# Per-head sums of squares of six batches in four 32-column matmul tiles, one activation, and a spread over partitions by transfers, in a linear attention and gated convolution kernel

## The chip, the cores and the metric

The kernel runs on one core of one Trainium2 chip. The metric is the device time of one execution in microseconds (us); lower is better. TensorE is called PE below, VectorE DVE, ScalarE ACT, GpSimd POOL and SyncE SP, as the profile does. PE's results land in PSUM, from which DVE and ACT take them to SBUF; transfers are issued by SP (plain copies and transposes) and by POOL (loads that change the type).

## The reference

There are 8 batches, 8 heads, 576 rows and 64 columns per head.

```python
kv  = einsum('bhsd,bhse->bhde', k, v)            # per head 64 x 64
o   = einsum('bhsd,bhde->bhse', q, kv)
rms = sqrt(mean(o * o, axis=-1, keepdims=True) + 1e-06)      # per batch, head and row
x   = o / rms * g_norm                            # then heads side by side: (8, 576, 512)
x1, x2, x3 = split(x @ w_proj, 3, axis=-1)
conv = irfft(rfft(x2, axis=1) * rfft(filter_fft, axis=0), n=576, axis=1)
out  = (x1 * conv * x3) @ w_out
```

The change touches how `1 / rms` comes about: it is one number for each batch, head and row, and it multiplies the 64 columns of that head.

## The kernel before

Everything is bf16 on PE with sums in float32. A batch is held with the 512 columns (8 heads of 64) on partitions, as four column blocks j = 0 to 3 of 128 partitions, so two heads lie in one block, and with the 576 rows along the free dimension in two halves of 288 (`TH`). The steps of a batch b, by the names that the code gives them:

- `K` sums k and v to kv, `eK` brings it to SBUF; `Qt` transposes q by a transfer of SP's (line 405; the first two batches use PE, `T0` and `T1`), and `Qh` is a tiny copy on POOL that waits for it.
- `O01` and `O23` (line 454) are attention outputs, two blocks each, in PSUM. ACT squares them (`sq`, line 464) and copies them with the gain g (`ob`, line 471; `ov` on DVE in batch 0).
- `R0` to `R3` (line 461) sum the squares of each head: two matmuls of 288 columns for each block, with `ind`, a 128 x 128 matrix of two blocks of ones, as weights. So the sum of a head appears on all of its 64 partitions. `rs0` to `rs3` (line 475, ACT) turn it to 1/rms in the tile `rstd`. `x0` and `x1` (line 489, DVE) multiply two blocks each of `o` by `rstd`; `x0` needs blocks 0 and 1, `x1` blocks 2 and 3.
- `Ga` and `Gb` (line 627) are the projections for x1 and x3, eight matmuls of 288 columns for each of four blocks, `x1n` and `gn` their evictions on ACT (633) and DVE (635). `fd`, `fr`, `fa` fold x on DVE, `rrM`, `rrT`, `abM`, `abT` project the folded x2 (lines 530 to 550), `F0` to `F2t` transform it, `M0` to `M2` (602, 617) multiply by the filter's spectrum, `A0`, `A1` (608) add products on POOL, `Av` on DVE. `Io`, `I`, `os`, `u`, `w`, `fin` transform back and multiply by the gates, `U`, `U4`, `ot` (750, 763, 754) apply `w_out` and store by transfers of SP's (757, 770).

All steps of all batches stand in one string, `ORDER`, each word a step and a batch (`R2.5` is step R2 of batch 5; a third number is a count of idle matmuls ahead of it). A loop walks it and each step issues its instructions on its engines, so the string sets the order on every engine and in every queue. Batches overlap: the attention part of batch b+1 runs among the convolution of batch b. Four tiles of two PSUM banks go round (`take` and `free`), and `sq`, `o` and `rstd` exist once each, so a batch's `rstd` may be written only when `x0` and `x1` of the batch ahead have read it. SP and POOL have semaphores for eight transfers each, so a transfer waits for the one eight ahead of it in its queue.

Of the kernel before, what the change touches and what calls it, by code (L numbers as in the profile page):

```python
# [19 lines left out]
ORDER = """Z.0 Zi.0 Lg.0 Lkb.0 Zt.0 Lq.0 Lvb.0 Lva.0 An.0 Lka.0 Zd.0 Zf.0 Lf.0 Tg.0 Zp.0 T0.0.20 Act.0 eTv0.0 T1.0 Lw1.0 Kb.0  # L20
eKb.0 Tb2.0 eTv1.0 Tb1.0 Lq.1 Lw2.0 Tb0.0 O23.0 sq2.0 Ka.0 R2.0.1 sq3.0 eKa.0 ov2.0 O01.0 rs2.0 ov3.0 sq1.0 R3.0 ov1.0
sq0.0 R1.0.1 rs3.0 rs1.0 x1.0 R0.0 ov0.0 rs0.0 x0.0 Ff2.0 Ff0.0 fd0.0 Ff1.0 Ga0.0 fr0.0 fr1.0 Lw3.0 fa0.0 Ga1.0 x11.0
Lv.1 fd1.0 x10.0 H1.0 H0.0 rrM.0 Lk.1 fa1.0 T0.1 rrT.0 err.0 eTa0.1 H2.0 Gb1.0 HN0.0 HN1.0 abM.0 F0.0 Gb0.0 eab.0 g1.0
K.1 M0.0 T1.1 abT.0 Lk.2 g0.0 eK.1 O01.1 eTa1.1 eT.0 sq0.1 ob0.1 F2.0 F2t.0 M2.0 sq1.1 Ga2.0 Lv.2 Lq.2 x12.0 Gb2.0
ob1.1 R1.1 g2.0 rs1.1 F1.0 R0.1 F1t.0 O23.1 rs0.1 sq2.1 Ga3.0 ob2.1 sq3.1 M1.0 R2.1 rs2.1 x0.1 ob3.1 x13.0 Av1.0 A0.0
Gb3.0 g3.0 R3.1 rs3.1 Lq.3 Qt.2 K.2 eK.2 Io01.0 I01.0 x1.1 Ga1.1 fd.1 Ga0.1 os01.0 u01.0 x11.1 Io23.0 O01.2 fr.1 x10.1
os23.0 sq0.2 I23.0 sq1.2 rrM.1 Qh.2 ob0.2 u23.0 ob1.2 Qt.3 R0.2 fa.1 rs0.2 w.0 rrT.1 err.1 O23.2 fin.0 abM.1 sq2.2
ob2.2 F0.1 eab.1 sq3.2 abT.1 eT.1 Gb1.1 Gb0.1 ob3.2 F1.1 M0.1 g1.1 R2.2 F1t.1 Lv.3 g0.1 rs2.2 Lk.3 R3.2 Ga3.1 rs3.2
R1.2 x13.1 Lwo.0 K.3 Lk.4 rs1.2 M1.1 Gb3.1 A0.1 x1.2 F2.1 Lv.4 x0.2 eK.3 A1.1 O23.3 F2t.1 g3.1 sq3.3 sq2.3 M2.1 fd.2
fa.2 U0.0 Io01.1 ob3.3 ob2.3 os01.1 ot0.0 Ga2.1 I01.1 x12.1 Gb2.1 R3.3 Io23.1 u01.1 rs3.3 g2.1 os23.1 I23.1 O01.3  # L30
abM.2 Lq.4 u23.1 w.1 sq1.3 sq0.3 Qh.3 Lq.5 Ga0.2 fin.1 ob1.3 ob0.3 abT.2 eab.2 x10.2 Ga1.2 R1.3 eT.2 fr.2 R0.3 x11.2
Gb1.2 rs1.3 F1.2 R2.3 rs0.3 F1t.2 g1.2 rrM.2 rs2.3 F2.2 rrT.2 K.4 M1.2 Qt.4 Lk.6 F2t.2 U2.0 eK.4 Lv.6 Lk.5 Lv.5 err.2
x1.3 Ga3.2 x0.3 M2.2 O23.4 ot2.0 x13.2 F0.2 sq3.4 sq2.4 ob2.4 Lq.6 ob3.4 fr.3 U0.1 M0.2 Qt.5 Gb0.2 R2.4 g0.2 Gb3.2
ot0.1 rs2.4 A1.2 A0.2 R3.4 g3.2 rrM.3 rs3.4 Io01.2 rrT.3 I01.2 os01.2 err.3 I23.2 Ga2.2 Gb2.2 fd.3 x12.2 fa.3 u01.2
g2.2 Io23.2 os23.2 u23.2 abM.3 abT.3 U4.1 eab.3 Ga0.3 ot4.1 F1.3 eT.3 w.2 fin.2 x10.3 O01.4 sq1.4 ob1.4 Qh.4 F1t.3
M1.3 sq0.4 U2.1 Ga1.3 ob0.4 ot2.1 F0.3 K.5 x1.4 A1.3 x11.3 F2.3 Gb0.3 eK.5 F2t.3 M0.3 R0.4 g0.3 Ga2.3 rs0.4 x12.3 R1.4
Gb2.3 M2.3 O23.5 rs1.4 Gb1.3 g2.3 x0.4 sq3.5 A0.3 sq2.5 ob3.5 ob2.5 U0.2 Io01.3 I01.3 Qt.6 fd.4 g1.3 fa.4 Ga3.3 os01.3
Gb3.3 x13.3 u01.3 Io23.3 g3.3 fr.4 abT.4 ot0.2 O01.5 os23.3 I23.3 eT.4 sq0.5 ob0.5 u23.3 Lk.7 abM.4 sq1.5 K.6 ob1.5
w.3 Ga0.4 eab.4 F1.4 R2.5 eK.6 x10.4 F1t.4 rs2.5 R3.5 rs3.5 rrM.4 R0.5 rs0.5 F2.4 fin.3 M1.4 x1.5 rrT.4 F2t.4 err.4
Ga1.4 R1.5 Gb1.4 M2.4 x11.4 Lv.7 rs1.5 O23.6 g1.4 sq3.6 F0.4 U2.2 sq2.6 ob3.6 Qh.5 Ga3.4 M0.4 ob2.6 ot2.2 O01.6 x13.4  # L40
Gb3.4 sq1.6 x0.5 Gb0.4 ob1.6 A1.4 g3.4 sq0.6 R3.6 ob0.6 A0.4 rs3.6 g0.4 U4.3 Ga2.4 ot4.3 R2.6 Gb2.4 fr.5 x12.4 rs2.6
fd.5 Io01.4 R1.6 I01.4 g2.4 os01.4 rrM.5 Io23.4 rs1.6 rrT.5 u01.4 os23.4 err.5 K.7 x1.6 I23.4 R0.6 Zn.0 fa.5 u23.4
abM.5 abT.5 rs0.6 eK.7 eab.5 U2.3 Lq.7 F0.5 Ga0.5 Qt.7 ot2.3 w.4 F1.5 fin.4 eT.5 F2.5 x10.5 M0.5 A0.5 F1t.5 U0.4 x0.6
M1.5 ot0.4 F2t.5 M2.5 A1.5 U0.3 Gb0.5 ot0.3 O23.7 sq3.7 g0.5 Ga1.5 Gb1.5 ob3.7 x11.5 fd.6 Io01.5 Ga2.5 fa.6 sq2.7 g1.5
I01.5 ob2.7 Ga3.5 os01.5 Io23.5 fr.6 x12.5 x13.5 Gb3.5 u01.5 Gb2.5 I23.5 os23.5 g3.5 g2.5 abM.6 Ga0.6 u23.5 eab.6
x10.6 O01.7 sq0.7 abT.6 ob0.7 eT.6 sq1.7 w.5 rrM.6 ob1.7 F1.6 Qh.6 rrT.6 F2.6 F1t.6 fin.5 err.6 F2t.6 U0.5 M1.6 Ga1.6
A1.6 F0.6 ot0.5 R2.7 M2.6 R1.7 x11.6 rs2.7 Gb0.6 U4.5 rs1.7 M0.6 R0.7 Gb1.6 A0.6 ot4.5 g0.6 R3.7 rs0.7 Ga2.6 U2.4
rs3.7 g1.6 I01.6 x12.6 Io01.6 Gb2.6 ot2.4 x1.7 Ga3.6 x0.7 fr.7 os01.6 u01.6 g2.6 rrM.7 fd.7 fa.7 x13.6 Io23.6 I23.6
os23.6 Gb3.6 g3.6 rrT.7 Ga1.7 err.7 abM.7 x11.7 u23.6 eab.7 F0.7 Ga0.7 x10.7 abT.7 w.6 F1.7 M0.7 eT.7 fin.6 Gb0.7 g0.7
F1t.7 F2.7 Ga2.7 x12.7 A0.7 F2t.7 Gb1.7 M1.7 U2.5 Av1.7 Qh.7 M2.7 g1.7 U2.6 Gb2.7 vae0.6 Io01.7 vve1.6 I01.7 ot2.5  # L50
g2.7 dse0.6 Ga3.7 dge1.6 J3.7 os01.7 x13.7 uj3.7 J2.7 dge2.6 uj2.7 U0.6 Gb3.7 u01.7 w01.7 dae3.6 fin01.7 wo23.7 wm23.7
Vq0.7 ot0.6 U4a.7 g3.7 fo23.7 U4b.7 vau.7 fm23.7 dsu2.7 Vq2.7 Vp0.7 dgu1.7 vaq0.7 vvq1.7 dsu0.7 dgu3.7 Vp2.7 dgq1.7
dsq0.7 dsq2.7 vap0.7 daq3.7 vvp1.7 dgp3.7 dap1.7 dsp0.7 dgp2.7"""


@with_exitstack
def kernel(
# [400 lines left out]
    def R(b, j):  # L458
        r2 = tmp['r', b, j] = take(("r", b, j))
        for h in range(2):  # L460
            nc.tensor.matmul(r2[:, h, 0:TH], ind, sq()[:, j, h * TH:(h + 1) * TH], start=True, stop=True)  # L461
# [416 lines left out]
```

## Time and profile before

| | us |
|---|---|
| median of 3 runs | 218.33 (218.29 to 219.61) |
| the profiled execution | 219.81 |
| its span, first to last instruction | 218.0 |
| PE busy in it | 200.0 |
| DVE, ACT, POOL busy in it | 184.0, 147.4, 68.1 |
| mean granted PE clock | 0.987 |

The profiled execution took 1.81 us more than its span and 1.48 us more than the median. A row of the timeline gives start and duration of neighbouring equal instructions (x8 is eight of them), their line and tiles, and in brackets how long their engine had stood idle and what ended it. Matmuls are pipelined: the start of the next row, not the end of the last, tells how long a row kept PE.

### The profile page before, as it was taken

Reading aid. Unit: us, or ns where it says so; the run is one execution under the profiler, and the core shown is the slowest. Engines: PE = TensorE matmul, PEld = TensorE weight load, DVE = VectorE, ACT = ScalarE, POOL = GpSimd, SP = SyncE. Lnnn points to the kernel's source line nnn. Section 1 sums busy time; section 2 is a strip of 40 time slices with the busy share of each in tenths; the row PEclk is TensorE's granted clock in tenths of the full one; section 3 lists DMA queues with packets and bytes.
Section 4 is the critical chain, followed back from the end, with each engine's and each line's share of the span. In section 5 each row is a group of like instructions: output and inputs, shape, how many; then the busy total and the mean of one; then the engine's idle time right before and its main releaser. Section 6 shows DMA issues by size and latency. Waiting matters only on the chain.

```text
span 218.0 us, 4583 instructions
## 1 busy us (share of the span) xinstructions
PE 200.0 (92%) x1825; PEld 123.2 (57%) x1848; DVE 184.0 (84%) x275; ACT 147.4 (68%) x232; POOL 68.1 (31%) x67
## 2 busy tenths in 40 slices
...
GB/s 64 203 208 206 205 204 203 187 182 163 205 174 146 230 86 146 230 156 191 240 147 188 121 0 98 154 115 96 164 32 0 38 111 96 0 3 18 178 205 132
DMA packets 40810, 30.12 MB, mean 138 GB/s; under 512 B 15796, under 2 KB 36276, under 8 KB 40788
## 3 DMA queue, kind: packets, MB, share of 16 engines
...
q8 instruction: 14, 0.23, 0.4%
...
HBM read 33.69 MB, written 9.44 MB: 198 GB/s over the span
## 4 chain that ended last, share of the span: by engine, by line
PE 69%; DVE 15%; DMA 5%; issue 3%; ACT 3%; POOL 1%; POOLq 0%; DVEq 0%; ACTq 0%
PE ps L627 24%; PE ps L750 10%; PE ps L544 5%; DMA wp<-in_moe_w_proj_dram 5%; DVE tpw L602 4%; PE ps L654 4%; PE ps L530 3%; PE ps L550 3%; PE ps L461 3%; PE ps L380 2%; PE ps L537 2%; PE ps L454 2%; PE ps L763 1%; PE ps L569 1%; PE ps L576 1%
## 5 line engine op out<-in xcount | busy, mean ns | idle before, releaser
L627 PE MATMUL ps<-x,wp 128*128 128x288 bf16 x512 | 72.5, 288 | 2.9 <-DVE tpw L602 2.4
L608 POOL TENSOR_TENSOR Y<-tpw 97x1024 bf16<-97x1024 f32 (+1 forms) x14 | 36.9, 2638 | 100.9 <-DVE tpw L602 100.8
L627 PEld LDWEIGHTS <-wp 128*128 128x128 bf16 x512 | 48.9, 98 | 21.5 <-issue 6.0
L602 DVE TENSOR_TENSOR tpw<-ps,HH 97x2048 f32<-97x2048 f32 (+1 forms) x16 | 36.6, 2288 | 3.6 <-PE ps L583 1.9
L635 DVE TENSOR_TENSOR g<-ps,x 128x576 bf16<-128x576 f32 x32 | 24.0, 753 | 8.3 <-PE ps L627 6.5
L475 ACT ACTIVATE rstd<-ps,bias_eps 128x576 bf16<-128x576 f32 x32 | 23.1, 748 | 7.5 <-PE ps L461 7.5
L633 ACT CAST x<-ps 128x576 bf16<-128x576 f32 x32 | 20.5, 644 | 10.9 <-PE ps L627 10.4
L750 PE MATMUL ps<-wo,yg 128*128 128x512 bf16 x106 | 26.0, 379 | 0.6 <-DVE g L635 0.2
L554 ACT CAST x<-ps 128x1024 bf16<-128x1024 f32 (+1 forms) x24 | 21.0, 874 | 8.2 <-PE ps L544 5.2
L464 ACT ACTIVATE sq<-ps 128x576 bf16<-128x576 f32 x32 | 20.1, 657 | 1.8 <-PE ps L454 1.6
L471 ACT ACTIVATE o<-ps,g_col 128x576 bf16<-128x576 f32 x28 | 20.3, 753 | 0.0
L754 ACT COPY ot<-ps 128x1024 f32<-128x1024 f32 x13 | 13.2, 1018 | 7.9 <-PE ps L750 7.8
L750 PEld LDWEIGHTS <-yg 128*128 128x128 bf16 x112 | 10.7, 98 | 12.1 <-issue 0.5
L654 PE MATMUL ps<-IV,Y 128*128 128x192 bf16 x120 | 15.6, 246 | 0.0
L544 PE MATMUL ps<-wp,ab 128*128 128x512 bf16 x58 | 14.8, 379 | 0.4
L663 DVE TENSOR_TENSOR u<-ps,os 128x576 bf16<-128x576 f32 x15 | 11.3, 754 | 3.1 <-ACT os L658 1.5
L461 PE MATMUL ps<-sq,ind 128*128 128x288 bf16 x64 | 13.0, 291 | 0.9 <-DVE o L469 0.5
L658 ACT COPY os<-ps 128x576 f32<-128x576 f32 x15 | 9.6, 642 | 5.5 <-PE ps L655 3.8
L655 PE MATMUL ps<-IV,Y 97*128 97x96 bf16 x60 | 12.4, 207 | 0.0
L489 DVE TENSOR_TENSOR x<-o,rstd 128x1152 bf16<-128x1152 bf16 x16 | 11.8, 750 | 0.7 <-ACT rstd L475 0.6
L386 ACT CAST kvblk<-ps 64x256 bf16<-64x256 f32 (+2 forms) x25 | 8.8, 353 | 4.5 <-PE ps L380 4.3
L654 PEld LDWEIGHTS <-Y 128*128 128x128 bf16 x120 | 9.6, 98 | 3.3 <-issue 1.1
...
## 6 DMA issues: line engine op xcount, KB each, us to landing
out_dram<-ot SPq DMA_DIRECT2D x54, 128.0 KB, 2.4
...
vb<-in_v_dram POOLq DMA_DIRECT2D x7, 576.0 KB, 10.7
kb<-in_k_dram POOLq DMA_DIRECT2D x7, 576.0 KB, 12.2
wp<-in_moe_w_proj_dram POOLq DMA_DIRECT2D x3, 512.0 KB, 11.4
...
```

The lines of the kernel that those rows point to most:

```text
L464: act.activation(out=halves(sq()[:, j]), in_=tmp['o', b, j][:, :, 0:TH], func=AF.Square)
L471: act.activation(out=by_time(osb(), j), in_=i_, func=AF.Copy, scale=g_col)
L475: act.activation(out=by_time(rstd(), j), in_=by_row(tmp['r', b, j]), func=AF.Abs_reciprocal_sqrt, scale=1.0 / D, bias=bias_eps)
L544: nc.tensor.matmul(pp[:, h], abt()[:, j, 2 * h * P:(2 * h + 1) * P], w2(j), start=(j == 0), stop=(j == NDC - 1))
L554: act.copy(out=o_(), in_=tmp[key, b])
L602: vec.tensor_mul(out=t_[:n], in0=xp[:n].unsqueeze(1).to_broadcast([n, 2, 2, DM]), in1=two)
L608: op(out=Yt()[:n, 2 * g:2 * g + 2], in0=t_[:n, ::-1, 0], in1=t_[:n, ::-1, 1])
L627: nc.tensor.matmul(pp[:, h, 0:TH], w_, x[:, j, h * TH:(h + 1) * TH], start=(j == 0), stop=(j == NDC - 1))
L633: act.copy(out=x1, in_=pp[:, :, 0:TH])
L635: vec.tensor_mul(out=halves(g13t()[:, dc]), in0=pp[:, :, 0:TH], in1=x1)
L654: nc.tensor.matmul(pp[:, i, 0:SB], Y[:, 2 * g + h, cs], IV[:, 2 * g + h, 0:SB], start=(g == 1), stop=(g == 2))
L750: nc.tensor.matmul(pp[:, cc], ygt(b)[:, dc, b % 2 * 64 + c * P:b % 2 * 64 + (c + 1) * P], wo[:, dc], start=(dc == 0), stop=(dc == NDC - 1))
```

## The change

For batches 1 to 6 the four pairs of `R` matmuls and the four `rs` activations are replaced. `Rc` issues eight matmuls with `ind32`, 128 x 32 weights whose 16 left columns are ones for the upper head and whose 16 right columns are ones for the lower; block j goes to column tile 32j of PE and to partitions 32j to 32j+31 of one PSUM tile. So all eight heads stand in one PSUM tile, 16 equal partitions each. `rsc` is one activation over it to the new tile `rc`. Then `sp0` to `sp3` spread it: for each head, one transfer on SP's queue reads one partition of `rc` 64 times over and writes 64 partitions of `rstd` (576 bf16 each, 73.7 KB), two for each block and eight for each batch, 48 in all. Batches 0 and 7 keep `R` and `rs`. `ORDER` is another string throughout; the loads of batch 1's q, k and v now stand ahead of those of `w_proj`.

```diff
-eKb.0 Tb2.0 eTv1.0 Tb1.0 Lq.1 Lw2.0 Tb0.0 O23.0 sq2.0 Ka.0 R2.0.1 sq3.0 eKa.0 ov2.0 O01.0 rs2.0 ov3.0 sq1.0 R3.0 ov1.0
+sq2.0 eTv0.0 ov3.0 Lka.0 Lva.0 Lq.1 R3.0.1 rs3.0 ov2.0 Tb0.0 Ff1.0 Ff0.0 Ka.0 eKa.0 Tb1.0 R2.0 Lk.1 Lv.1 rs2.0 Zp.0
...
+    ind32 = consts.tile([P, 32], BF16)
...
+        vec.memset(ind32, 0.0)
+        for h in range(2):
+            vec.memset(ind32[64 * h:64 * h + 64, 16 * h:16 * h + 16], 1.0)
...
+    rc = lambda: buf("rc", 0, [P, S])
+
+    @one
+    def Rc(b):
+        r2 = tmp['rc', b] = take(("rc", b))
+        for h in range(2):
+            for j in range(NDC):
+                nc.tensor.matmul(r2[32 * j:32 * j + 32, h, 0:TH], ind32, sq()[:, j, h * TH:(h + 1) * TH], start=True, stop=True,
+                                 tile_position=(0, 32 * j))
+
+    @one
+    def rsc(b):
+        act.activation(out=rc().rearrange("p (m a r) -> p a m r", m=3, a=2), in_=by_row(tmp['rc', b]),
+                       func=AF.Abs_reciprocal_sqrt, scale=1.0 / D, bias=bias_eps)
+        free(("rc", b))
+
+    def spread(b, j):
+        for hp in range(2):
+            r = rc()[32 * j + 16 * hp:32 * j + 16 * hp + 1]
+            nc.sync.dma_start(out=rstd()[64 * hp:64 * hp + 64, j:j + 1], in_=bass.AP(tensor=r.tensor, offset=r.offset, ap=[list(r.ap[0]), [0, 64], [1, S]]))
+
+    for j in range(NDC):
+        step["sp%d" % j] = lambda b, j=j: spread(b, j)
```

PE in batch 5, before: the sums of one block stand between other matmuls, and the other blocks' pairs follow some steps on (`sq` are the squares, `ind` the ones; `x_481,FY` is part of `F1` of batch 4).

```order
L576 MATMUL ps_69<-x_481,FY 128x512
L461 LDWEIGHTS ind
L461 MATMUL ps_67<-sq,ind 128x288
L461 LDWEIGHTS ind
L461 MATMUL ps_67<-sq,ind 128x288
L583 LDWEIGHTS FZ
```

After, at the same place (lines have moved by 32): all eight stand in one run, each of 32 output partitions, behind `abT` (`wp,ab`) and ahead of `F1` (`x_620,FW`) of batch 4. Two of the eight are shown.

```order
L582 MATMUL ps_66<-wp,ab 128x512
L478 LDWEIGHTS ind_83
L478 MATMUL ps_69<-sq,ind_83 32x288
...
L478 LDWEIGHTS ind_83
L478 MATMUL ps_69<-sq,ind_83 32x288
L608 LDWEIGHTS FW
L608 MATMUL ps_68<-x_620,FW 128x512
```

So four short stretches of full-width matmuls became one stretch per batch, for which PE changes to 32-column tiles and back.

SP before, from the queue's start: the transposes of q of batches 2 and 3 stand ahead of everything, then stores.

```order
L182 DMA g_row<-in_g_norm_dram 1x2x64
L405 DMA_TRANSPOSE qT<-qb_74 128x24x96 [waits DMASW6_49,DVE_49,PE_49]
L405 DMA_TRANSPOSE qT<-qb_75 128x24x96 [waits DMASW7_49,DVE_49,PE_49]
L757 DMA out_dram<-ot 64x1x512 [waits Activation_49]
```

After, from the last spread of batch 1 on: the transpose for batch 2, then the four transfers of `sp3` and `sp2` of batch 2, then the transpose for batch 3 (it waits for POOL's load of q), and only behind it `sp1` and `sp0` of batch 2.

```order
L490 DMA rstd<-rc 64x1x576 [waits DMAHW0_49]
L413 DMA_TRANSPOSE qT<-qb_74 128x24x96 [waits DMAHW1_49,DMASW3_49,PE_49]
L490 DMA rstd<-rc 64x1x576 [waits DMAHW2_49,Activation_49]
L490 DMA rstd<-rc 64x1x576 [waits DMAHW3_49]
L490 DMA rstd<-rc 64x1x576 [waits DMAHW4_49]
L490 DMA rstd<-rc 64x1x576 [waits DMAHW5_49]
L413 DMA_TRANSPOSE qT<-qb_75 128x24x96 [waits DMAHW6_49,DMASW0_49,PE_49]
L490 DMA rstd<-rc 64x1x576 [waits DMAHW7_49,DVE_49]
L490 DMA rstd<-rc 64x1x576 [waits DMAHW0_49]
L490 DMA rstd<-rc 64x1x576 [waits DMAHW1_49]
L490 DMA rstd<-rc 64x1x576 [waits DMAHW2_49]
L789 DMA out_dram<-ot 64x1x512 [waits DMAHW3_49,Activation_49]
```

So the second half of batch 2's `rstd` moved behind a transpose and its load.

DVE where batch 1's x is made, before: both parts of x follow `M1` or a gate of batch 0, next to the activations that feed them.

```order
L602 TENSOR_TENSOR tpw<-ps_66,HH 128x2048
L489 TENSOR_TENSOR x<-o,rstd 128x1152
L608 TENSOR_TENSOR Y<-tpw 128x1024
L635 TENSOR_TENSOR g_532<-ps_66,x_432 128x576
L489 TENSOR_TENSOR x<-o,rstd 128x1152
```

After: two gates and `M0` of batch 0 stand between the activation `rsc` of batch 1 and its first x, which now waits for four transfers, and `M1` of batch 0 (L634, 128x2048), `M2` (L649) and gates stand behind it.

```order
L667 TENSOR_TENSOR g_631<-ps_66,x_557 128x576
L667 TENSOR_TENSOR g_631<-ps_67,x_547 128x576
L634 TENSOR_TENSOR tpw<-ps_68,HH 97x2048
L521 TENSOR_TENSOR x<-o,rstd 128x1152
L634 TENSOR_TENSOR tpw<-ps_67,HH 128x2048
L649 TENSOR_TENSOR Y<-ps_69,HM 128x1024
L640 TENSOR_TENSOR Y<-tpw 128x1024
L667 TENSOR_TENSOR g_631<-ps_68,x_547 128x576
L521 TENSOR_TENSOR x<-o,rstd 128x1152
```

So x moved away from the activation that feeds it, and a wait there now holds up products of the batch ahead.

More of the change, by code (lines that the diff above doesn't have):

```diff
@@ L24 @@
[L24 to L53, printed above, removed]
+ORDER = """Z.0 Lg.0 Lkb.0 Lq.0 Zi.0 Lvb.0 Zt.0 Zd.0 T0.0.22 An.0 Lf.0 Act.0 Zf.0 T1.0 Kb.0 Tg.0 eKb.0 eTv1.0 Tb2.0 O23.0 sq3.0
@@ new lines @@
+sq2.0 eTv0.0 ov3.0 Lka.0 Lva.0 Lq.1 R3.0.1 rs3.0 ov2.0 Tb0.0 Ff1.0 Ff0.0 Ka.0 eKa.0 Tb1.0 R2.0 Lk.1 Lv.1 rs2.0 Zp.0
+Ff2.0 O01.0 T1.1 sq1.0 eTa1.1 Lw1.0 sq0.0 ov1.0 ov0.0 Lw2.0 H2.0 T0.1 R1.0 rs1.0 eTa0.1 H1.0 x1.0 fd1.0 R0.0 K.1 eK.1
+rs0.0 x0.0 H0.0 O01.1 sq0.1 Ga0.0 sq1.1 ob0.1 fd0.0 ob1.1 fa1.0 x10.0 Ga1.0 x11.0 fa0.0 O23.1 Lq.2 sq3.1 Lw3.0 fr0.0
+sq2.1 fr1.0 ob2.1 abM.0 ob3.1 Rc.1 rrM.0 rrT.0 rsc.1 Gb1.0 err.0 HN0.0 Gb0.0 g1.0 eab.0 g0.0 sp3.1 F0.0 abT.0 F2.0
+HN1.0 sp2.1 sp1.1 Lv.2 F1.0 M0.0 eT.0 sp0.1 F1t.0 F2t.0 Qt.2 Lk.2 x1.1 Ga2.0 x12.0 M1.0 A0.0 Ga3.0 x13.0 Lv.3 Gb2.0
@@ new lines @@
+M2.0 K.2 Av1.0 g2.0 Gb3.0 Io01.0 x0.1 eK.2 O01.2 os01.0 g3.0 I01.0 sq0.2 Lq.3 ob0.2 Ga1.1 sq1.2 u01.0 ob1.2 fr.1 x11.1
+Io23.0 os23.0 Ga0.1 fd.1 x10.1 O23.2 I23.0 rrM.1 sq3.2 u23.0 rrT.1 sq2.2 Qh.2 ob2.2 Rc.2 ob3.2 fa.1 Lwo.0 Gb1.1 w.0
+rsc.2 abM.1 sp3.2 abT.1 fin.0 err.1 sp2.2 eab.1 F0.1 Qt.3 Lk.3 F1.1 eT.1 g1.1 Ga3.1 x13.1 F1t.1 M0.1 K.3 F2.1 A0.1
+eK.3 Gb0.1 M1.1 F2t.1 g0.1 Ga2.1 Gb2.1 x12.1 sp1.2 M2.1 g2.1 O23.3 sq3.3 U0.0 x1.2 sq2.3 sp0.2 ob3.3 A1.1 Io01.1 ob2.3
+I01.1 Io23.1 os01.1 Gb3.1 x0.2 fd.2 ot0.0 Ga1.2 u01.1 g3.1 O01.3 os23.1 fa.2 x11.2 I23.1 u23.1 sq0.3 sq1.3 abM.2 ob0.3
```

39 lines of the change are left out of this document (31 added, 8 removed).

## The prediction

> **What bounds the kernel now.** I read the page's busy times first, then the chain that ended last, then the busy times by stretches.
>
> ```profile
> span 218.0 us, 4583 instructions
> PE 200.0 (92%) x1825; PEld 123.2 (57%) x1848; DVE 184.0 (84%) x275; ACT 147.4 (68%) x232; POOL 68.1 (31%) x67
> PE 69%; DVE 15%; DMA 5%; issue 3%; ACT 3%; POOL 1%; POOLq 0%; DVEq 0%; ACTq 0%
> ```
>
> PE is busy for 92% of the span and is 69% of the chain. The stretches (length, then PE, PEld, DVE, ACT and POOL busy, then PE's clock, DMA share and GB/s) show where that holds:
>
> ```profile
> 13.00:25.00 12.00, 9.63 (x114) 5.16 (x112) 10.24 (x28) 10.17 (x18) 5.66 (x8) 1.00 1.21 205
> 45.00:55.00 10.00, 9.19 (x123) 5.92 (x117) 9.78 (x18) 9.44 (x18) 3.26 (x5) 1.00 1.17 181
> 85.00:95.00 10.00, 7.67 (x50) 4.66 (x48) 7.73 (x9) 4.87 (x8) 4.15 (x3) 0.83 1.23 207
> 165.00:175.00 10.00, 9.95 (x69) 5.29 (x68) 8.34 (x7) 8.21 (x12) 2.37 (x1) 1.00 0.15 36
> ```
>
> From about 95 us on PE has 9.95 of 10 us: a microsecond of PE work taken out there is a microsecond of span. Between 45 and 55 us DVE has 9.78 of 10 and PE has gaps, with the transfer engines full (1.17 of their time): there DVE and transfers count. The stretch at 85 us holds one accident, used below.
>
> **The removed matmuls.** The first row is PE's group of `R`, the second ACT's group of `rs`.
>
> ```profile
> L461 PE MATMUL ps<-sq,ind 128*128 128x288 bf16 x64 | 13.0, 291 | 0.9 <-DVE o L469 0.5 <-ACT rstd L475 0.3
> L475 ACT ACTIVATE rstd<-ps,bias_eps 128x576 bf16<-128x576 f32 x32 | 23.1, 748 | 7.5 <-PE ps L461 7.5
> ```
>
> 291 ns is the latency of one matmul; what a pair keeps PE from is read off the starts in the timeline:
>
> ```profile
> 68.67 0.41 PE L461 MATMUL ps<-sq,ind 128*128 128x288 bf16 x2
> 68.92 0.33 PE L654 MATMUL ps<-IV,Y 128*128 128x192 bf16 x2
> ```
>
> A pair takes 68.92 - 68.67 = 0.25 us, four pairs 1.00 us. `Rc` also has eight matmuls of 288 columns, in two rounds of four column tiles. Do four such tiles run side by side? The filter's folding (L305) issues 32-column tiles of 512 columns already:
>
> ```profile
> 19.40 0.40 PE L305 MATMUL ps<-fn,rev 96*32 96x512 bf16 x4
> 19.62 0.40 PE L305 MATMUL ps<-fn,ident 96*32 96x512 bf16 x4
> ```
>
> Four start every 0.21 us, 0.41 ns a column, so two rounds of 288 take 0.24 us. But PE must change its tiling and back:
>
> ```profile
> 62.12 1.16 PE L627 MATMUL ps<-x,wp 128*128 128x288 bf16 x8
> 63.20 0.41 PE L590 MATMUL ps<-x,FZ 128*64 128x512 bf16 x2
> 63.54 0.44 PE L454 MATMUL ps<-qT,kvblk 64*64 64x288 bf16 x8
> ```
>
> Eight gate matmuls keep PE for 0.98 us (the chain, below), so the tiled L590 could start at 63.10 and starts at 63.20: 0.10 lost going in. Its two run side by side, 0.21 us, so the next could start at 63.41 and starts at 63.54: 0.13 lost. `Rc` costs 0.24 + 0.23 = 0.47 us for 1.00, and six batches save 6 x 0.53 = 3.2 us. The bounds: without the two changes 6 x 0.76 = 4.6 us saved; if tiles do not overlap, 8 x 0.125 + 0.23 = 1.23 us, 1.4 us lost over six batches. I take 3.2, since the fold is the same tile width. The Trainium skill, TensorEngine Tiling (Array Packing), Key Properties, says that changing the tiling mode drains TensorE; by that the 0.23 belongs in, and the two gaps agree. Taken without it the sum would be 4.6.
>
> **The removed activations.** 18 x 0.748 = 13.5 us leave ACT. ACT is 68% busy and PE waited for `rstd` only twice (0.3 us each, in the waits), so PE's work hides them: 0, bound 0.6 us gained. A gain for DVE or PSUM beyond that I cannot see in the waits.
>
> **The transfers.** 48 new ones on SP, where before only stores and transposes were: first stores (duration on SP, then time to landing), then transposes, then stores while loads fill the engines, then the transfer rate between 116 and 130 us in 40 slices.
>
> ```profile
> L757 SPq DMA_DIRECT2D out_dram<-ot x52: 315/462/1310, 68.1 to 208.2; - x52
> DMA to landing us min/median/max: 1.9/2.4/11.0
> ...
> L405 SPq DMA_TRANSPOSE qT<-qb x6: 3006/3940/8513, 41.8 to 141.9; - x6
> DMA to landing us min/median/max: 4.9/7.3/19.0
> ...
> out_dram<-ot SPq DMA_DIRECT2D x4, 128.0 KB, 6.4
> ...
> GB/s 184 184 193 187 204 208 200 195 208 208 208 208 259 388 411 357 217 47 12 23 6 0 0 0 0 0 0 0 0 0 0 0 0 0 0 0 0 0 0 0
> ```
>
> No row has a copy from SBUF to SBUF. The nearest are the stores: 0.46 us of SP each and 2.4 us to land, 6.4 among loads. So the first two blocks of `rstd` are there 0.75 (`rsc`) + 4 x 0.46 + 2.4 = 5.0 us after the matmuls, all four after 6.8. What DVE still has to do in that time, in its program order, by these durations:
>
> ```profile
> L602 DVE TENSOR_TENSOR tpw<-ps,HH 97x2048 f32<-97x2048 f32 (+1 forms) x16 | 36.6, 2288 | 3.6 <-PE ps L583 1.9 <-PE ps L569 1.3
> L635 DVE TENSOR_TENSOR g<-ps,x 128x576 bf16<-128x576 f32 x32 | 24.0, 753 | 8.3 <-PE ps L627 6.5 <-ACT rstd L475 0.8 <-ACT ot L754 0.5
> L675 DVE TENSOR_TENSOR yg<-w,g 128x2304 bf16<-128x2304 bf16 (+1 forms) x8 | 10.3, 1283 | 0.2
> L617 DVE TENSOR_TENSOR Y<-ps,HM 128x1024 bf16<-128x1024 f32 x8 | 9.7, 1218 | 1.1 <-PE ps L594 0.8 <-PE ps L454 0.3
> L489 DVE TENSOR_TENSOR x<-o,rstd 128x1152 bf16<-128x1152 bf16 x16 | 11.8, 750 | 0.7 <-ACT rstd L475 0.6
> 66.45 0.98 PE ps L627 x8
> ```
>
> - Batch 1, `x1`: two gates and `M0`, 2 x 0.75 + 2.29 = 3.8 us. The transfers are 1.2 us late, by the 6.4 us row 5.2 late. `M1`, `M2` and gates of batch 0 wait behind x on DVE. PE has three more gate halves ahead of needing them (`Ga2`, `Ga3`, `Gb2`, 2.9 us by the last row), which cover the 1.2 and leave 2.3 of the 5.2. I charge 0.5, nearer the store without loads, since one of these moves 73.7 KB and a store 128.
> - Batch 2, `x0`: `fin`, `M0`, `M1`, `M2`, three gates and `x1` = 1.3 + 4.6 + 1.2 + 2.3 + 0.75 = 10.1 us. Its transfers stand behind the transpose for batch 3: 0.75 + 4 x 0.46 + 3.9 + 4 x 0.46 + 2.4 = 10.8, late by 0.7; with 8.5 for the transpose 15.4. PE has five gates (4.9 us) and, in `U`, `abM` and `abT`, 20 matmuls of 512 columns at 0.21 (4.2 us) between `Rc` and the first gate that needs x, and `K`, `O23`, five `F` steps and three inverse steps of less than a gate each, in all about 14 us as an estimate. So I charge 0; bound 1.4 us, and more where the transpose itself lands late (a rival).
> - The other batches have 5.6 us of DVE work or more (batch 5: `fin`, `M1`, `M2` and a gate) for the 5.0: 0. If all lag, what is late next is `fd`, `fr`, `fa`, then `rrM` on PE.
> - Loads: 48 x 73.7 KB = 3.5 MB more for engines that move about 205 GB/s when full. Up to 100 us that is 3 batches' worth, 8.6 us of transfer time; PE waited for no load after the first weights, so 0, bound 1 us lost.
>
> **The start.** `w_proj` now stands behind batch 1's k and v:
>
> ```profile
> 13.29 11.39 DMA wp<-in_moe_w_proj_dram
> ...
> 34.29 0.88 PE ps L380 x48
> 35.17 0.62 PE ps L417 x12
> ...
> 36.77 0.37 PE ps L454 x8
> ```
>
> Two loads of 576 KB at 205 GB/s are 5.8 us more before the weights land. In exchange PE does batch 1's `K` (0.88), `T1` (0.62), `O01` and `O23` (0.37 each), `Rc` (0.47) and batch 0's `abM` (8 x 0.21) ahead of the first `Gb`: 4.4 us that came later before, and it had 12 - 9.63 = 2.4 us of idle time in that stretch. I charge 0, bounds 2 us either way.
>
> **The sum.** -3.2 + 0.5 = -2.7 us. The profiled execution takes 219.81, so 217.1; the median is 1.48 lower, and by the same step 218.33 - 2.7 = **215.6 us**. 1% (2.2 us) is what a measurement of this kernel can tell from no change: faster is below 216.1, slower above 220.5.
>
> **Rivals.**
>
> 1. *One partition is a narrow source.* Each spread reads one partition; no row here does. If that goes at one engine's rate, 411 GB/s / 16 = 26 GB/s, 73.7 KB take 2.9 us, and two that hinder each other 5.7. Then x is ready after 0.75 + 1.84 + 5.7 = 8.3 us: `x1` of batch 1 late by 4.5 (1.6 uncovered), of batch 5 by 2.7, `x0` of batch 2 by 4; with the cover that PE has left I charge 3 more: 218.6, within 1%. The Trainium skill, SBUF - State Buffer, Door 1, says that a transfer's rate depends on how many of 16 ports its partitions reach, and its map puts the sources of blocks 2 and 3 on two ports; at its 435 GB/s over 16 ports that is an estimate of 5.4 us for the four that `x1` needs. Nothing here tests it.
> 2. *Slower: the transpose blocks SP.* One transpose landed after 19.0 us. If batch 3's does, and batch 2's last transfers stand behind it in the ring, `x0` is ready after 0.75 + 1.84 + 19 = 22 us against PE's 14: PE stands 8 us, and then runs slowly, as here:
>
> ```profile
> 83.67 3.52 DVE L509 TENSOR_TENSOR rr<-x 128x384 bf16<-128x384 bf16 x2
> 84.33 2.36 POOL L608 TENSOR_TENSOR Y<-tpw 128x1024 bf16<-128x1024 f32 x1
> 89.44 1.92 PE L627 MATMUL ps<-x,wp 128*128 128x288 bf16 x8 [2.12 <-DVE tpw L602]
> ```
>
>    After 2.12 us of waiting eight gate matmuls take 1.92 us instead of 0.98, and the granted clock of that stretch is 0.83: 1.7 us more. So up to 215.6 + 9.7 = 225; slower from a PE stall of 3.2 us on, a landing of 14.2 us. I put it at 222.
> 3. *More than the matmuls.* The accident above is that two short DVE sums took 3.52 us while POOL's sum of 2.36 us ran, and PE waited 2.12 for DVE. If the new order never meets the like, 2.1 + 1.7 = 3.8 us more go: 211.8. Against it speaks that the median run is already 1.48 us shorter than this one, so it may not have all of it.
> 4. *Tiles do not overlap*: +1.4 + 0.5, 220.2. The fold rows speak against it.
>
> **Chances.** The forecast 0.47 (its own range 213.6 to 217.3; three quarters of it below 216.1), rival 1 0.20, rival 2 0.18, rival 3 0.13, rival 4 0.02. Faster: 0.35 + 0.13 = 0.48; within 1%: 0.12 + 0.17 + 0.01 = 0.30; slower: 0.18 + 0.03 + 0.01 = 0.22. The range runs from rival 3's 211.8 to 221.5, short of most of rival 2.
>
> **What would show it.** PE: eight `Rc` matmuls about 0.47 us from the first start to the next step's, with ACT's `rsc` x6 at 0.75. The transfers: landing 2.4 us right, above 5 rival 1. DVE waits for transfers at `x1` of batch 1 (about 1 us) and nowhere else; a wait at `x0` of batch 2 with the transpose in front and a clock below 1 is rival 2. I am wrong altogether if PE is no longer above 9.9 of 10 us after 95 us.

## The result, and the profile after

The changed kernel takes 255.99 us (median of 4 runs, 255.02 to 256.93), the kernel before 218.36 beside it: ratio 1.171, 95% interval 1.165 to 1.177, so 37.6 us slower. The forecast was 215.6 us, and its range ended at 221.5. (Where some executions of a kernel below took over 1.5% longer than its fastest, its time and ratio are those of the others, and the range of all stands beside.)

The page of the kernel after: span, busy times, PE and its clock in 40 slices, the chain that ended last.

```profile
span 255.2 us, 4674 instructions
PE 209.5 (82%) x1829; PEld 122.9 (48%) x1849; DVE 184.0 (72%) x278; ACT 136.2 (53%) x214; POOL 67.4 (26%) x67
PE   7689879536996479954999889699979999999980
PEclk9965999985999959995799979979999999999996
PE 40%; DMA 25%; DVE 14%; ACT 7%; issue 5%; SPq 5%; POOL 1%; POOLq 0%; DVEq 0%; ACTq 0%
PE ps L659 13%; DMA rstd<-rc 12%; DMA qT<-qb 10%; PE ps L576 5%; SPq L490 5%; PE ps L782 4%; DVE tpw L634 4%; PE ps L686 3%; DMA vb<-in_v_dram 3%; DVE g L667 2%; PE ps L462 2%; PE ps L313 2%; PE ps L562 2%; ACT o L503 2%; DVE u L695 1%
```

PE was 69% of the chain and is 40%. A quarter of the chain is transfers, and two kinds have nearly all of it: the new `rstd<-rc` with 12%, and the transposes `qT<-qb`, which the change did not touch, with 10%. PE's busy time is 9.5 us longer for less work: its clock is below full in many slices.

The same stretches as in the prediction's second fence, in the kernel after (length; PE, PEld, DVE, ACT, POOL busy; PE's clock; DMA share; GB/s):

```profile
13.00:25.00 12.00, 11.19 (x114) 5.21 (x108) 4.93 (x13) 8.15 (x15) 3.54 (x5) 0.58 1.31 204
45.00:55.00 10.00, 5.73 (x86) 4.29 (x85) 7.44 (x8) 3.02 (x6) 3.86 (x3) 1.00 1.02 109
85.00:95.00 10.00, 4.63 (x26) 2.57 (x28) 6.41 (x10) 3.00 (x5) 0.00 (x0) 0.76 1.23 214
165.00:175.00 10.00, 8.87 (x59) 5.53 (x60) 8.57 (x11) 6.59 (x10) 3.97 (x4) 0.83 0.88 128
```

PE loses at three kinds of place: at the start it runs at 0.58 of its clock; in the middle it stands for half of a stretch; at 165 us it still lacks a tenth. After the last spread (186.9 us) it is full from 195 us on: 9.95 of 10 us to 205, and again to 215.

The transfers by their line: duration on SP (ns), who waited for them (us, times), landing.

```profile
L490 SPq DMA_DIRECT2D rstd<-rc x48: 469/604/1655, 39.8 to 186.9; - x48
  DVE x L521: 20.6, 6
DMA to landing us min/median/max: 4.4/5.3/8.7
```

The transposes in the same way:

```profile
L413 SPq DMA_TRANSPOSE qT<-qb x6: 3066/5854/6691, 47.1 to 191.1; - x6
  PE ps L462: 14.0, 3
DMA to landing us min/median/max: 5.0/9.1/12.9
```

`Rc` of batch 2 in PE's timeline with the row behind it, and `rsc` by its line:

```profile
67.06 0.43 PE L478 MATMUL ps<-sq,ind 128*32 128x288 bf16 x8 [0.16 <-DVE u L696]
67.42 1.16 PE L659 MATMUL ps<-x,wp 128*128 128x288 bf16 x8
...
L483 ACT ACTIVATE rc<-ps,bias_eps x6: 742/750/835, 38.9 to 176.1; 128x576 bf16<-128x576 f32 x6
```

`Rc` keeps PE 67.42 - 67.06 = 0.36 us and `rsc` takes 0.75, as forecast. The transfers land after 5.3 us where 2.4 was taken. The transposes take 5.85 us of SP (3.94 before) and land after 9.1 (7.3 before).

The chain between 39 and 60 us:

```profile
39.09 0.64 ACT rc L483
39.75 0.58 SPq L490
40.39 0.58 SPq L490
41.01 1.66 SPq L490
42.71 4.40 DMA rstd<-rc
47.11 12.63 DMA qT<-qb
59.87 0.69 PE ps L462 x8
```

Batch 2's `rsc` and its two x, from the timelines of ACT and DVE:

```profile
67.53 0.74 ACT L483 ACTIVATE rc<-ps,bias_eps 128x576 bf16<-128x576 f32 x1
78.93 0.79 DVE L521 TENSOR_TENSOR x<-o,rstd 128x1152 bf16<-128x1152 bf16 x1
87.96 0.76 DVE L521 TENSOR_TENSOR x<-o,rstd 128x1152 bf16<-128x1152 bf16 x1 [8.24 <-DMA rstd<-rc]
```

The transpose for batch 2 started only at 47.11, when a spread of batch 1 had landed, and PE had `qT` at 59.87. Batch 2's second x came 20.4 us after its `rsc`, with the transpose for batch 3 between its two pairs of spreads on SP.

### The profile page after: what moved, and what is told of

It reads as the page before. It is cut to its first block, busy times and chain, and to the rows that moved or that the text cites. A ratio compares the mean times of both kernels' runs of the same rounds, so it can differ in the third digit from the quotient of the medians.

```text
span 255.2 us, 4674 instructions
## 1 busy us (share of the span) xinstructions
PE 209.5 (82%) x1829; PEld 122.9 (48%) x1849; DVE 184.0 (72%) x278; ACT 136.2 (53%) x214; POOL 67.4 (26%) x67
## 3 DMA queue, kind: packets, MB, share of 16 engines
q1 hardware_dynamic: 23012, 15.34, 39.3%
## 4 chain that ended last, share of the span: by engine, by line
PE 40%; DMA 25%; DVE 14%; ACT 7%; issue 5%; SPq 5%; POOL 1%; POOLq 0%; DVEq 0%; ACTq 0%
PE ps L659 13%; DMA rstd<-rc 12%; DMA qT<-qb 10%; PE ps L576 5%; SPq L490 5%; PE ps L782 4%; DVE tpw L634 4%; PE ps L686 3%; DMA vb<-in_v_dram 3%; DVE g L667 2%; PE ps L462 2%; PE ps L313 2%; PE ps L562 2%; ACT o L503 2%; DVE u L695 1%
## 5 line engine op out<-in xcount | busy, mean ns | idle before, releaser
L659 PE MATMUL ps<-x,wp 128*128 128x288 bf16 x512 | 74.8, 297 | 9.2 <-DVE x L521 4.8
L659 PEld LDWEIGHTS <-wp 128*128 128x128 bf16 x512 | 50.1, 101 | 29.2 <-issue 8.0
L634 DVE TENSOR_TENSOR tpw<-ps,HH 97x2048 f32<-97x2048 f32 (+1 forms) x16 | 36.4, 2283 | 1.8 <-PE ps L615 1.2
L521 DVE TENSOR_TENSOR x<-o,rstd 128x1152 bf16<-128x1152 bf16 x16 | 15.7, 980 | 20.7 <-DMA rstd<-rc 20.6
L665 ACT CAST x<-ps 128x576 bf16<-128x576 f32 x32 | 20.4, 644 | 18.5 <-PE ps L659 13.4
L586 ACT CAST x<-ps 128x1024 bf16<-128x1024 f32 (+1 forms) x24 | 20.6, 872 | 15.3 <-PE ps L576 7.2
L695 DVE TENSOR_TENSOR u<-ps,os 128x576 bf16<-128x576 f32 x15 | 11.3, 756 | 21.4 <-PE ps L687 19.4
L462 PE MATMUL ps<-qT,kvblk 64*64 64x288 bf16 x128 | 8.5, 340 | 16.5 <-DMA qT<-qb 14.0
L686 PE MATMUL ps<-IV,Y 128*128 128x192 bf16 x120 | 17.4, 264 | 2.4 <-DVE u L696 2.2
L576 PE MATMUL ps<-wp,ab 128*128 128x512 bf16 x57 | 16.4, 411 | 0.9 <-DVE ab L546 0.3
L462 PEld LDWEIGHTS <-kvblk 64*64 64x64 bf16 x128 | 2.8, 113 | 21.7 <-issue 11.5
L687 PE MATMUL ps<-IV,Y 97*128 97x96 bf16 x60 | 13.1, 218 | 0.0
```

The lines of the kernel that those rows point to most:

```text
L462: nc.tensor.matmul(op[64 * hp:64 * hp + 64, r, 0:TH], kvblk[b % 2][64 * r:64 * r + 64, r ^ hp, j], qT(b)[64 * r:64 * r + 64, 6 * j + 3 * h ...
L576: nc.tensor.matmul(pp[:, h], abt()[:, j, 2 * h * P:(2 * h + 1) * P], w2(j), start=(j == 0), stop=(j == NDC - 1))
L586: act.copy(out=o_(), in_=tmp[key, b])
L634: vec.tensor_mul(out=t_[:n], in0=xp[:n].unsqueeze(1).to_broadcast([n, 2, 2, DM]), in1=two)
L659: nc.tensor.matmul(pp[:, h, 0:TH], w_, x[:, j, h * TH:(h + 1) * TH], start=(j == 0), stop=(j == NDC - 1))
L665: act.copy(out=x1, in_=pp[:, :, 0:TH])
```

## The experiments

Three theories stood at first: Q, the spreads and the transposes hold each other up on SP; O, the new order is worse in itself; L, x waits for the spreads wherever they are issued.

**New order, no transfers.** The 24 words `sp*` leave `ORDER`; x of batches 1 to 6 is scaled by batch 0's `rstd`.

> The changed kernel in its own order, with Rc and rsc, but without the 48 transfers: x of batches 1 to 6 is multiplied by the 1/rms that batch 0 left, so the output is not the reference's. Theory Q (the loss is SP's queue and what stands in it: spreads of 0.6 us each and transposes behind each other, so that q of the next batch and rstd come late): back to 214 to 219 us, no PE wait on qT. Theory O (the new order by itself is worse, transfers or not): 240 or more.

222.0 us (nine of ten executions; all 219.8 to 224.4), ratio 1.012 (1.009 to 1.016), above the 214 to 219 of Q. So 34.0 of the 37.6 us are the transfers, and the new order with `Rc` costs 3.7 where the forecast's terms without the transfers gave 3.2 of gain. O is refuted as the main cause. (x waits for no sums at all here, so this prices the order from below.) The stretch from 17 to 25 us in this kernel:

```profile
17.00:25.00 8.00, 8.00 (x84) 3.83 (x78) 3.18 (x10) 5.03 (x8) 1.55 (x2) 0.50 1.30 203
```

One of PE's first waits and two rows of the folds, from its timeline:

```profile
12.85 0.44 PE L460 MATMUL ps<-qT,kvblk 64*64 64x288 bf16 x8 [1.08 <-ACT kvblk L392]
16.56 0.65 PE L311 MATMUL ps<-fn,rev 96*32 96x512 bf16 x4
16.99 0.65 PE L311 MATMUL ps<-fn,ident 96*32 96x512 bf16 x4
```

Four folds start every 0.43 us instead of 0.21. Behind waits of no more than 1.1 us each (PE is busy for 0.51 of the 2 us from 12 to 14) it runs at half its clock for about 10 us, from 15.7 on; in the kernel before the clock is 1.00 there.

**New order with the old sums.** `Rc.b` and `rsc.b` become `R3 rs3 R2 rs2 R1 rs1 R0 rs0` on one spot, without transfers.

> The new order with the four pairs of R and four rs per batch put back where Rc and rsc stood, one pair behind the other, and no spreads; the output is the reference's. Theory Q: 219 to 226 us (the 3 us of matmuls are back, and pairs in a row wait a little for each other's PSUM). Theory O: 245 or more.

228.1 us (two of four; all 227.1 to 231.9), ratio 1.042 (1.033 to 1.051), above the 219 to 226 of Q. Eight steps on one spot wait for each other (PE 2.9 us in all for ACT's `rs`), so this prices that spot and not the order.

**Spreads issued by ACT.**

```diff
-            nc.sync.dma_start(out=rstd()[64 * hp:64 * hp + 64, j:j + 1], in_=...)
+            nc.scalar.dma_start(out=rstd()[64 * hp:64 * hp + 64, j:j + 1], in_=...)
```

> The changed kernel with the 48 spreads issued by ACT instead of SP, so that transposes and stores stand alone in SP's queue. Theory Q: PE no longer waits for qT, 225 to 238 us, with some 20 us more ACT time for issuing. Theory L (the latency of a spread, 5.3 us, at x is the loss, whatever queue it is in): 248 or more, with DVE's 20 us of waits for rstd unchanged. Theory O: 250 or more.

258.3 us (three of four; all 257.8 to 264.5), ratio 1.179 (1.173 to 1.185). The waits of x and the landing of the spreads in this kernel:

```profile
  DVE x L521: 26.5, 7
DMA to landing us min/median/max: 4.2/5.3/8.9
```

PE no longer waits 14.0 us for `qT`, x waits 26.5 instead of 20.6, and the time is nearly the same. A queue of their own doesn't land the spreads sooner, as L says. It is no clean test of Q, since the issues now stand on ACT and are 8% of the chain there.

**Old order with `Rc` and the spreads.** `R*` and `rs*` of batches 1 to 6 become `Rc`, `rsc`, `sp3` to `sp0`, and `x1` of batch 4 moves behind them; all else stands as before.

> The order of before with only R and rs of batches 1 to 6 replaced by Rc, rsc and the spreads at the place of the first R behind the last square. Transposes keep their places, x stands right behind the spreads. Theory Q: PE waits little for qT, but x has little cover: DVE waits 3 to 6 us per batch, 230 to 245 us. Theory L: like that or worse, 240 to 260. Theory O: 222 or less.

287.62 us, ratio 1.314 (1.307 to 1.320), above all the ranges; DVE waits 55.9 us at x. With these transfers the old order is 31.6 us slower than the new one, which thus hides part of their price; it isn't the fault.

**Why do the spreads take 5.3 us?** Three kernels change the transfers alone (count, queue and order stay); part of the rows of `rstd` is then wrong or old. First 64 source partitions, each read once:

```diff
-            r = rc()[32 * j + 16 * hp:32 * j + 16 * hp + 1]
...
+            nc.sync.dma_start(out=rstd()[64 * hp:64 * hp + 64, j:j + 1], in_=rc()[64 * hp:64 * hp + 64].unsqueeze(1))
```

> The changed kernel with each transfer reading 64 partitions of rc once each instead of one partition 64 times: same 48 transfers, 64 rows of 1152 bytes each, same queue, same order. (The rows that were not meant for it go into rstd, so batches 1 to 6 are scaled by wrong values; only the time counts.) Changed kernel: landing 5.3 us, 0.60 us of SP each, 256.0 us; without the transfers 222.0. Theory P (one partition is a narrow source): landing falls to about 2.4 to 3 us, SP's share to about 0.46, and the time to 225 to 240. Theory D (64 short rows are what costs) and Theory B (73.7 KB are what costs): landing stays at 5 us or above, the time at 252 to 258.

Half of the columns (`[0, 64], [1, S // 2]`):

> The changed kernel with each transfer moving only the first 288 of 576 columns: 48 transfers of 64 rows of 576 bytes, half the bytes, same rows, still from one partition. (The other half of rstd keeps batch 0's values.) Theory P: what exceeds a store's 2.4 us, 2.9 us, goes to half: landing about 3.9 us, time about 240. Theory B the same. Theory D: landing stays at 5.3 us and the time at 252 to 258.

Half of the destination partitions (`[0, 32], [1, S]`):

> The changed kernel with each transfer filling only 32 of its 64 destination partitions: 48 transfers of 32 rows of 1152 bytes, half the bytes and half the rows, still from one partition. (The other 32 keep batch 0's values.) Theories P, B and D: landing about 3.9 us, time about 240. If landing and time stay, neither bytes nor rows set them, and the price is a fixed one per transfer or the order of the queue.

The landing lines of the three, in this order:

```profile
DMA to landing us min/median/max: 1.9/2.9/6.7
```

```profile
DMA to landing us min/median/max: 2.8/3.0/6.3
```

```profile
DMA to landing us min/median/max: 2.8/3.0/6.5
```

The times are 221.6 us (one of four; all 221.6 to 232.1), 225.9 (one of four; all 225.9 to 232.3) and 226.1 (226.0 to 228.7; ratio 1.035, 1.028 to 1.042); one execution says little, and the argument rests on the landings. The same 64 rows and 73.7 KB land in 2.9 us from 64 partitions and in 5.3 from one: neither the rows nor the bytes are the price, but the one partition. Halving what is taken from it, by columns or by rows, brings 3.0, less than the 3.9 expected. An estimate from the shortest landings: 36.9 KB more take 4.4 - 2.8 = 1.6 us, 23 GB/s out of one partition; rival 1 had 26.

**One partition, or one way out of SBUF?** `rc` holds each head's sums on 16 partitions, so several can serve as source without a change of the result (`n` and `step` stand for the numbers given below).

```diff
+            src = bass.AP(tensor=r.tensor, offset=r.offset, ap=[[step * r.ap[0][0], n], [0, 64 // n], [1, S]])
+            nc.sync.dma_start(out=rstd()[64 * hp:64 * hp + 64, j:j + 1], in_=src)
```

Four neighbours (n 4, step 1):

> The changed kernel, each transfer reading the first 4 of the 16 partitions that hold the same sums (neighbours, 16 times each) instead of one partition 64 times; the result is the same, the 64 rows, bytes, queue and order too. Theory P1 (reading one partition over and over is what is slow): 16 readings of a partition instead of 64, landing falls from 5.3 to about 3 us and the time to 222 to 232. Theory P2 (neighbouring partitions share one way out of SBUF, so the number of such ways counts): landing stays at about 5.3 us and the time at 252 to 258.

Every fourth (n 4, step 4):

> As the run before, but the 4 partitions are every fourth of the 16. P1 and P2 both: landing about 3 us and the time 222 to 232. If only this one of the two is fast, P2 is shown; if neither is, 4 partitions are still narrow and the cause is another.

All 16 (n 16, step 1):

> As the two runs before, with all 16 partitions, each read 4 times. P1 and P2: landing 2.9 to 3 us as with 64 partitions, transposes landing at about 6.2 instead of 9.1 us, no wait of PE for qT, time 221 to 232. This is the changed kernel mended, with the reference's result; by the forecast's other steps it would stand at 215.6, by the runs without transfers at 222 or above.

286.84 us (ratio 1.306, 1.296 to 1.316), 245.78 (1.121, 1.112 to 1.131) and 230.7 (two of four, 229.0 and 232.4; all 229.0 to 237.5; 1.052, 1.040 to 1.063). The SP rows and the page's packets of the first, the SP rows of the second, then SP, landing and packets of the third (the trace has no landing of the first two's spreads):

```profile
L491 SPq DMA_DIRECT2D rstd<-rc x48: 537/1158/2495, 40.7 to 216.2; - x48
  DVE x L522: 51.0, 9
q1 hardware_dynamic: 22436, 15.34, 28.5%
```

```profile
L491 SPq DMA_DIRECT2D rstd<-rc x48: 537/540/2319, 37.9 to 173.8; - x48
  DVE x L522: 9.2, 5
```

```profile
L491 SPq DMA_DIRECT2D rstd<-rc x48: 545/592/1292, 37.8 to 158.6; - x48
DMA to landing us min/median/max: 2.3/2.8/6.5
q1 hardware_dynamic: 23012, 15.34, 31.4%
```

From 16 partitions the transfers land in 2.8 us, and x waits 5.4 us instead of 20.6. The two kernels with four sources are the ones to compare with each other: each partition is read 16 times in both, so P1 (the count of readings) can't tell them apart, and the far four are 41 us faster. Which partitions they are counts, as P2 says. By the Trainium skill, SBUF - State Buffer, Door 1, four neighbouring partitions share one of 16 ports, and every fourth partition reaches another. The far four being faster than the near four agrees with it.

Against one partition (256.0 us) or 16 these two are no clean comparison, and P2's 252 to 258 and 222 to 232 missed both. Four sources in the pattern changed something else too: the queue has 23012 - 22436 = 576 packets fewer at the same bytes, 12 for each of the 48 transfers, and in the trace, while any is, on average only 2.7 (near) and 3.4 (far) of their 1152-byte packets are under way at a time, against 10.7 from one partition and 8.4 from 16. So these transfers went about four packets abreast instead of up to sixteen, which fits four neighbours being slower than one partition and the far four slower than 16. Whether one partition is narrow by itself or by what it shares with its neighbours no run at the full width tells.

**What remains with 16 partitions.** The start first: four idle matmuls ahead of the first O step, three instead of one ahead of the first `R3` (`O23.0.4`, `R3.0.3`), in the order without transfers:

> The new order without the 48 transfers (x of batches 1 to 6 scaled by batch 0's rstd), with four idle matmuls ahead of the first O step and three instead of one ahead of the first R3, where PE waits 1.1 and 0.6 us. Without them 222.0 us, with the granted clock at 0.50 between 17 and 25 us. Theory S (the start's half clock is part of what the new order costs): clock 1.00 there, and 2 to 4 us less, 218 to 220. Rival (the start waits for loads anyway, the first gate at 33.3 us for x): clock 1.00 there and the time still 221 to 223.

219.4 us (nine of ten; all 217.6 to 223.3), ratio 0.999 (0.995 to 1.003), 2.6 less than without them: S holds at its lower end. In the profiled execution, the longest of the ten, the clock is 0.94 in the stretch that had 0.50. But how long PE stays at half clock differs between executions of the same program: the kernels with four far and with 16 source partitions differ from the changed kernel in nothing before the first spread, at 38 us, and had 0.93 and 0.94 from 17 to 25 us when profiled. The idle matmuls with the 16 source partitions:

> The mended source (16 partitions, each read 4 times; 234.0 us, 229 to 238) with the idle matmuls at the start, which brought the order without transfers from 222.0 to 219.6. Theory A (the costs add): 229 to 232 us, 2 to 4 below 234.0. Theory L (what is left of the transfers is their latency and what it does to the clock, and the start is covered by it): 232 to 236, no gain.

231.1 us (230.6 to 233.3), ratio 1.055 (1.047 to 1.063), against 230.7 without them: no gain is shown, so that the costs add is not shown either. Most of what x waits here (6.1 of 10.7 us) is in one place, in batch 4, and the chain leads to it through SP:

```profile
85.94 21.80 DMA qT<-qb x2
107.75 6.16 DMA out_dram<-ot
113.93 5.10 DMA rstd<-rc
120.64 2.08 PE ps L659 x8
```

Two transposes (batches 4 and 5) and twelve stores stand on SP ahead of batch 4's spreads; PE waits 4.9 us for what x holds up, and then eight gate matmuls take 2.08 us. Next, the transposes for batches 2 and 3 ahead of the spreads (`Qt.2` ahead of `sp3.1`, `Qt.3` ahead of `sp3.2`):

> As the run before, with the transposes for batches 2 and 3 ahead of the spreads of batches 1 and 2 on SP instead of behind them. Theory Q2 (what is left over 219.6 us is the transposes that stand behind the spreads): no wait of PE for qT, 222 to 227 us. Theory L: the spreads stand behind the transposes instead, 3 to 4 us later, DVE waits longer at x of batches 1 and 2, and the time is that of the run before or 1 to 5 us above.

232.3 us (three of four; all 232.2 to 237.1), ratio 1.065 (1.052 to 1.077). x waits 12.2 us instead of 10.7, PE waits for `qT` in neither: the place of these two transposes is not it. Those for batches 4 and 5 were not moved. Then all the traffic and none of the waiting:

```diff
-            nc.sync.dma_start(out=rstd()[64 * hp:64 * hp + 64, j:j + 1], in_=src)
+            nc.sync.dma_start(out=buf("rstd2", 0, [P, NDC, S])[64 * hp:64 * hp + 64, j:j + 1], in_=src)
```

> The mended kernel with the warm start (231.1 us), its 48 transfers going into a tile of their own that nobody reads, while x of batches 1 to 6 reads batch 0's rstd: all the traffic, none of the waiting. Theory L (x waits for what is left of the latency, the clock falls after each wait): 219 to 222, as without transfers (219.6). Theory C (the transfers hinder the transposes, stores and loads beside them): 227 to 232, as with the waiting. Half way between says that each has its part.

219.6 us (one of four; all 219.6 to 229.1). The one execution stands where no transfers stand (219.4), as L says; the other three stand at 226 to 229, as C says. It decides nothing: how the 231.1 - 219.4 = 11.7 us divide between waiting at x and transfers that hinder others stays open. Last, the 16 partitions in the old order:

> The mended source in the order that was searched for the kernel before (287.6 us with one partition as source, 219.0 without transfers). Theory L (four transfers, 0.75 us of rsc, 4 x 0.6 of SP and 2.8 to land, are about 6 us, and x stands about 1 to 3 us behind the sums in this order): DVE waits at x some 3 to 5 us in each of six batches, 235 to 250 us, so the new order was needed to hide the transfers. Rival: with 2.8 us to land the old order hides them too, 219 to 225.

267.11 us, ratio 1.216 (1.207 to 1.226), above the 235 to 250 expected, x waiting 35.5 us: 5.9 us a batch with a landing of 2.5. An order with more work ahead of x was needed.

**The matmuls and activations alone.** The old order with `Rc` and `rsc` and no transfers; x of batches 1 to 6 is scaled by batch 0's `rstd`.

> The order of the kernel before with R and rs of batches 1 to 6 replaced by Rc and rsc, and no transfers: x of batches 1 to 6 is scaled by batch 0's rstd. It prices the removed matmuls and activations alone, in the order that was searched for the kernel before. The forecast's step: 3.2 us less than before, 215.1 us (bounds 213.7 to 219.7). If the 6.4 us by which the new order without transfers (222.0) missed its forecast are the new order's, this one is at 215 to 216; if Rc saves nothing, it is at 218 to 222 and the new order costs little.

218.97 us (217.82 to 220.64) against 219.7 beside it, ratio 1.001 (0.997 to 1.005): the 3.2 us are not there. The starts of the 13th, 25th and 61st group of eight gate matmuls on PE show where they go, in the profiled execution (220.64 us): 59.92, 100.96 and 194.26 us before, 59.03, 102.30 and 195.20 here. After two batches of `Rc` the kernel is 0.9 us ahead (2 x 0.53 were forecast); then this comes:

```profile
82.91 3.52 DVE L537 TENSOR_TENSOR x<-x,x 128x768 bf16<-128x768 bf16 x1
83.63 2.36 POOL L638 TENSOR_TENSOR Y<-tpw 128x1024 bf16<-128x1024 f32 x1
...
89.33 1.02 PE L560 MATMUL ps<-wp,rr 128*128 128x512 bf16 x4 [1.64 <-DVE tpw L632]
91.76 0.26 PE L685 MATMUL ps<-IV,Y 97*128 97x96 bf16 x1 [1.24 <-POOL Y L638]
94.93 3.65 PE L657 MATMUL ps<-x,wp 128*128 128x288 bf16 x16
```

A sum of DVE lasts 3.52 us beside POOL's (0.56 is its usual time), PE waits 1.64 for DVE and 1.24 for POOL, and then 16 gate matmuls take 3.65 us at a lowered clock, for 2.12 at the full one. The accident that the prediction met at 84 us in the kernel before is here too, and larger. Behind it, from the 25th to the 61st group, the kernel wins back 1.34 - 0.94 = 0.4 us where three batches of `Rc` were to win 1.6; PE waits 0.5 us for `rsc` there, and the rest is open.

## Why the prediction was wrong

From the forecast's point of view the 256.0 us come apart so, by differences of the times: one source partition instead of 16, 256.0 - 230.7 = 25.3 (up to 2.6 of it can be the start, whose clock happened to be higher in the profiled execution with 16); the transfers that remain, 230.7 - 222.0 = 8.7 (11.7 with the idle matmuls); the new order with `Rc`, 222.0 - 218.4 = 3.6, of which the start is 2.6. Without transfers and with the idle matmuls the kernel stands at 0.999 of the one before, where 3.2 us below it was forecast.

- **The transfers** are the step that failed. "I charge 0.5, nearer the store without loads, since one of these moves 73.7 KB and a store 128": size was the wrong measure of nearness. A store's 128 KB come from 64 partitions, the spread's 73.7 KB from one, and the landing was 5.3 us instead of 2.4. The rate of rival 1 (26 GB/s, 23 estimated from the landings) was about right, and a landing above 5 was its sign; it had chance 0.20.
- **The cover.** Rival 1 was priced at 3 us for the whole kernel, since only three batches were held to be late and PE to have other work. DVE waited at x in five of six batches, 20.6 us, and what is behind x on DVE (`M1`, gates, `u`) holds PE up too. The 0 for the other batches rested on 5.6 us of DVE work against 5.0 from `rsc` to landing, while that chain is 8.0 us for batch 1 (39.09 to 47.11).
- **The transposes.** Rival 2 came in addition, in the place that it named (second x of batch 2, after 20.4 us where 22 was said), but the near number is luck: no transpose landed after 19 us (12.9 at most), and the 20.4 are a transpose of 6.0 on SP, slower issues (2.7 and 3.9) and a landing of 6.9. PE stood 3.8 us there and not 8. It came in another place too: rival 2 looked at transposes in front of spreads, and the spreads in front of a transpose cost PE 6.5 us at 59.87. The step for SP counted its issue times and left out that a transfer waits for the one eight ahead.
- **The clock.** Some of these waits are followed by slow matmuls: behind the 6.5 us, eight matmuls that keep PE for 0.37 us in the kernel before kept it 60.50 - 59.87 = 0.63:

```profile
59.87 0.69 PE L462 MATMUL ps<-qT,kvblk 64*64 64x288 bf16 x8 [6.47 <-DMA qT<-qb]
60.50 0.50 PE L686 MATMUL ps<-IV,Y 128*128 128x192 bf16 x2
```

Behind another wait for `qT`, of 2.34 us, the same eight took 80.64 - 80.26 = 0.38, at the full clock:

```profile
80.26 0.44 PE L462 MATMUL ps<-qT,kvblk 64*64 64x288 bf16 x8 [2.34 <-DMA qT<-qb]
80.64 1.90 PE L782 MATMUL ps<-wo,yg 128*128 128x512 bf16 x8
```

So not every wait costs twice. The forecast counted the lowered clock only in its rivals.
- **The start**, charged 0 with bounds of 2 us either way: 2.6 us lost in the order without transfers, by the half clock and not by the loads, which the step looked at.
- **The removed matmuls**: `Rc` cost 0.36 us at the full clock where 0.47 was charged, and the saving of 0.5 us a batch is seen after two batches. That it reaches the end was wrong: in the profiled execution the collision of DVE and POOL and the clock behind it give back more than is saved, and later batches win little.
- **The removed activations**, 0: nothing contradicts it; ACT is busy 11 us less and nothing became faster.
- That PE is no longer above 9.9 of 10 us after 95 us was named as what would show the forecast wrong altogether; it had 8.87 at 165.
